# The two PSUM banks of y, split by token half instead of by channel half

## The chip, the cores and the metric

The kernel runs on one core of a Trainium2 chip. The metric is the device time of one execution in microseconds; the time given is the median of several executions. The profile beside it is that of one further execution, which has its own time.

## The reference

Two blocks follow each other. The first is a chunked state-space scan over 4 batches, 8 heads, 768 tokens, 32 channels a head and 16 states; the second mixes tokens through a low-rank product (rank 32) and then channels through two matrices with a ReLU between them. Cut to what matters here:

```python
for c in range(nc):                                  # chunks of 32 tokens
    M = einsum('bhin,bhjn->bhij', Cc, Bc) * L        # C B^T, decayed, causal
    y_intra = einsum('bhij,bhjd->bhid', M, xc)
    y_inter = einsum('bhin,bhnd->bhid', Cc, state) * decay_to_i
    y[chunk] = y_intra + y_inter
    state = decay_full * state + sum_j(Bc * xc * decay_from_j)
# mixer, on y as (batch, token, 256 channels)
u = y + (y^T U V)^T
out = u + relu(u w_ch1) w_ch2
```

## The kernel before

The kernel takes chunks of 64 tokens instead of 32. A block is 128 tokens, that is two token halves p of 64; a pair k of two blocks c is 256 tokens, and there are 12 pairs, three to a batch. All matrices are float32, and every matmul instruction leaves two records in the trace.

What is done, and in which order, is written out by hand in the string PLAN (lines 34 to 70): each word is a letter and its indices, and `follow` calls the function of that letter, so that the words give the order in which each engine gets its instructions. An engine works through its own queue in that order and waits where an operand is not there. Between the words of the scan stand those of the mixer (U, f, e, h, d, S, a, p, q) for the batch before, so that TensorE has matmuls of 128 rows and 128 columns to do meanwhile. The words B, X and w are loads issued by SyncE (SP); each is held until the last VectorE instruction that stands before it in PLAN is done, and the loads behind it in SP's queue wait with it.

The words that bear on y, for a pair k:

- `P`, `Q`: VectorE scales B and C with the decays into BC. `T`, `V`: TensorE transposes BC, ScalarE (or VectorE) copies the result into T and, masked by head, into Cm.
- `g` (`gram`, line 506): TensorE forms C B^T of the pair, 16 matmuls that use 32 rows of the array and 64 columns, into four banks (line 522). `m` and `M` (`mask`): VectorE cuts it to the causal part, M (through the helper's line, L174).
- `s` (`state`, line 546): TensorE forms B^T x per half block, 16 matmuls of 64 rows and 32 columns (line 556). `u` (`update`): VectorE carries the state S from half block to half block, GpSimd makes Sm of it, which is S masked by head.
- `n` (`intra(k, 0)`) and `j` (`crossed`, that is `intra(k, 1)`), line 680: the M x share of y, 32 matmuls of 64 rows and 32 columns, half of them in n and half in j.
- `i` (`inter`, `carried`, line 642): the states' share of y, C times Sm, 16 matmuls of 32 rows and 64 columns; 12 in the first pair of a batch, whose first half block has no state.
- `I` (`both`): i of pair k and g of pair k+1 in one word, their matmuls interleaved. PLAN has it for pairs 7, 9 and 10.
- `y` (`yout`): two ScalarE copies take y from PSUM into yT, which has channels on partitions and tokens in the free dimension. `t`, `O` (`ytokens`): TensorE transposes yT back (line 707), and the result goes into ytok.

y of a pair takes two PSUM banks. Bank n holds channel half n (heads 4n to 4n+3), and in its free dimension the two blocks, the two token halves and 64 tokens. A matmul whose operands lie on partitions 0 to 63 works in the upper rows of the array, one with operands on 64 to 127 in the lower rows. M x of token half p uses row half p. In the states' share the row half is the channel half n, since T and Sm have heads on partitions; so that share fits bank n as it is. Of M x, n does what lies straight (row half p into bank n = p), and j what lies crossed (row half p into bank n = 1 - p).

A crossed piece must not begin before the last straight matmul on these banks is done. The code keeps this order with a VectorE instruction that waits for the straight ones and that the first crossed matmul waits for: either one that does so in any case (`behind["part"]`), or a copy of one column into the tile settled that is there for nothing else (`apart`; for the last pair `settle`).

The first matmul into a bank and a group of 32 output partitions clears it (`fresh`, line 614); the later ones add.

Of the kernel before, what the change touches and what calls it, by code (L numbers as in the profile page):

```python
# [44 lines left out]
    'R4 e1.0.4 e1.0.1 f1.0.6 i6 h1.0.0 s7 R7 R6 X8 B8 j6 e1.0.5 d0.0.0.0 d0.0.0.1 d0.0.0.2 h1.0.4 '  # L45
    'u7 f1.0.7 e1.0.6 h1.0.1 h1.0.6 d0.0.0.3 T9 h1.0.5 T9 P8 d0.1.2.0 e1.0.7 h1.0.7 d0.1.2.1 f1.0.2 '
    'd0.1.1.0 e1.0.2 T8 f1.0.3 d0.1.1.1 d0.1.2.2 d0.1.2.3 e1.0.3 T8 y6 h1.0.2 h1.0.3 d0.1.1.2 '
    'd0.1.1.3 s8 u8 n7 I7 s9 j7 d1.0.0.0 d1.0.1.0 y7 m8 d1.0.0.1 d1.0.0.2 M8 d1.0.1.1 S1.1 f1.1.0 '
    'R5 d1.0.0.3 d1.0.1.2 R4 R6 X11 f1.1.7 R7 e1.1.0 h1.1.0 P11 d1.0.0.4 d1.0.1.3 d1.0.0.5 f1.1.6 '
    'e1.1.7 d1.0.1.4 u9 d1.0.2.0 d1.0.1.5 e1.1.6 h1.1.6 d1.0.2.1 f1.1.1 d1.0.2.2 d1.0.2.3 e1.1.1 '  # L50
    'h1.1.7 f1.1.4 t7 d1.0.2.4 d1.0.2.5 f1.1.3 e1.1.4 h1.1.1 f1.1.2 e1.1.3 f1.1.5 e1.1.2 h1.1.2 i8 '
    'n8 s10 j8 h1.1.3 h1.1.4 e1.1.5 d1.1.1.0 d1.1.0.0 d1.1.0.1 u10 d1.1.1.1 d1.1.1.2 d1.1.0.2 '
    'h1.1.5 d1.1.1.3 d1.1.0.3 d1.1.2.0 d1.1.2.1 d1.1.2.2 d1.1.2.3 y8 d1.1.0.4 d1.1.1.4 d1.1.1.5 '
    'd1.1.2.4 d1.1.2.5 d1.1.0.5 t8 t6 g9 T10 m9 T10 M9 p2 n9 I9 m10 q2 T11 T11 M10 j9 y9 a2.0 s11 '
    'u11 I10 m11 n10 S2.0 M11 t9 f2.0.0 f2.0.4 e2.0.0 h2.0.0 f2.0.1 f2.0.5 j10 e2.0.1 f2.0.2 y10 '
    'e2.0.5 h2.0.1 e2.0.4 h2.0.4 f2.0.3 h2.0.5 e2.0.2 i11 n11 e2.0.3 h2.0.2 h2.0.3 f2.0.6 f2.0.7 '
    'a2.1 e2.0.6 h2.0.6 j11 y11 S2.1 e2.0.7 d2.0.0.0 h2.0.7 t10 t11 d2.0.0.1 d2.0.0.2 f2.1.1 f2.1.0 '
    'd2.0.0.3 f2.1.3 e2.1.1 e2.1.0 d2.0.0.4 d2.0.0.5 p3 h2.1.0 f2.1.2 h2.1.1 d2.0.2.0 d2.0.1.0 '
    'e2.1.2 h2.1.2 d2.0.2.1 e2.1.3 h2.1.3 d2.0.1.1 d2.0.1.2 d2.0.2.2 d2.0.2.3 f2.1.5 f2.1.4 q3 '
    'e2.1.5 e2.1.4 d2.0.1.3 d2.0.2.4 h2.1.4 d2.0.2.5 d2.0.1.4 d2.0.1.5 f2.1.6 f2.1.7 h2.1.5 a3.0 '  # L60
    'e2.1.6 d2.1.0.0 e2.1.7 h2.1.6 a3.1 d2.1.2.0 d2.1.2.1 d2.1.0.1 d2.1.0.2 S3.0 f3.0.3 f3.0.2 '
    'h2.1.7 f3.0.0 d2.1.0.3 e3.0.3 f3.0.1 d2.1.0.4 d2.1.0.5 e3.0.2 h3.0.2 h3.0.3 e3.0.0 d2.1.1.0 '
    'd2.1.2.2 d2.1.2.3 d2.1.1.1 d2.1.1.2 f3.0.5 f3.0.4 d2.1.1.3 e3.0.1 h3.0.0 h3.0.1 d2.1.2.4 '
    'e3.0.5 f3.0.6 e3.0.4 d2.1.1.4 f3.0.7 d2.1.2.5 h3.0.4 e3.0.6 e3.0.7 h3.0.6 d2.1.1.5 d3.0.2.0 '
    'S3.1 d3.0.2.1 d3.0.0.0 d3.0.0.1 d3.0.0.2 f3.1.4 h3.0.5 f3.1.0 h3.0.7 d3.0.2.2 f3.1.5 e3.1.4 '
    'd3.0.2.3 e3.1.0 h3.1.0 f3.1.1 d3.0.2.4 d3.0.0.3 f3.1.2 d3.0.0.4 d3.0.0.5 d3.0.2.5 d3.0.1.0 '
    'h3.1.4 e3.1.5 h3.1.5 e3.1.1 h3.1.1 f3.1.6 d3.0.1.1 f3.1.3 e3.1.2 e3.1.6 d3.0.1.2 e3.1.3 h3.1.2 '
    'h3.1.3 d3.0.1.3 f3.1.7 d3.0.1.4 d3.0.1.5 h3.1.6 e3.1.7 d3.1.2.0 d3.1.2.1 d3.1.2.2 h3.1.7 '
    'd3.1.2.3 d3.1.1.0 d3.1.1.1 d3.1.2.4 d3.1.2.5 d3.1.1.2 d3.1.1.3 d3.1.0.0 d3.1.0.1 d3.1.0.2 '
    'd3.1.0.3 d3.1.1.4 d3.1.1.5 d3.1.0.4 d3.1.0.5 ')  # L70


@with_exitstack
def kernel(
# [27 lines left out]
    nc = tc.nc  # L102
    P = 128
# [13 lines left out]
    Q = 32  # L117
    H = 64
# [44 lines left out]
    class Kept:  # L163
# [6 lines left out]
        def __getattr__(self, name):  # L170
# [8 lines left out]
    vector = Kept(nc.vector)  # L179
# [7 lines left out]
        out=a_sb,  # L187
        in_=a.rearrange("(g b) h (c s) -> g (b h c) s", g=2, s=P).rearrange(
            "g r s -> r g s"))
# [322 lines left out]
    def opened(k, tags="xxzz"):  # L512

        st[k].setdefault("of", {})["g"] = behind["turn"]
        st[k]["g"] = four(tags, 2, 2, H)

    def crossing(k, c, p, of):

        s = st[k]
        for r in of:  # L520
            rows, cols = ts(r, Q), ts(p, H)
            nc.tensor.matmul(  # L522
                out=s["g"][r][cols, c], lhsT=s["T"][rows, 0, c, cols],
                rhs=s["Cm"][rows, :, :, ts(2 * c + p, Q)].rearrange("r v t i -> r v i t"),
                start=(c == 0), stop=True, skip_group_check=True)
# [67 lines left out]
    def apart(copy):  # L593

        behind["part"] = op = copy(out=settled, in_=slot[:, :1])
        for product in behind["first"]:
            tc.add_manual_dep(op.ins, product.ins.name, mybir.DependencyInfo(
                mybir.DependencyClass.Sync, mybir.DependencyReason.DATA))

    def settle():  # L600

        t = bank("x", P)
        nc.tensor.matmul(out=t, lhsT=ident, rhs=ident, start=True, stop=True)
        behind["part"] = vector.tensor_copy(out=settled, in_=t[:, :1])

    def channels(k):

        s = st[k]
        if "y" not in s:
            s["y"] = [bank("y", 2, 2, H) for n in range(2)]  # L610
            s["seen"] = set()
        return s["y"]

    def fresh(k, n, quadrants):

        new = {(n, i) for i in quadrants}
        seen = st[k]["seen"]
        assert new <= seen or not new & seen
        first = not new <= seen
        seen |= new  # L620
        return first

    def straight():

        behind.pop("part", None)
        behind["turn"] += 1

    def inter(k):

        channels(k)  # L630
        straight()
        for c in range(2):
            for p in range(2):
                carried(k, c, p, range(4))

    def carried(k, c, p, of):

        b, q = pairs[k]
        own = st.get(("Sm", b, 4 * q + 2 * c + p))
        assert own is not None or 4 * q + 2 * c + p == 0  # L640
        for r in of if own is not None else ():
            behind["first"].append(nc.tensor.matmul(  # L642
                out=channels(k)[r // 2][ts(r % 2, H), c, p], lhsT=own[ts(r, Q)],
                rhs=st[k]["T"][ts(r, Q), 1, :, ts(2 * c + p, Q)].rearrange("r t i -> r i t"),
                start=fresh(k, r // 2, range(2 * (r % 2), 2 * (r % 2) + 2)),
                stop=True, skip_group_check=True))

    def both(k):

        channels(k)  # L650
        straight()
        opened(k + 1)
        for c in range(2):
            for v in range(2):
                carried(k, c, 0, (v, v + 2))
                crossing(k + 1, 0, c, (1 - v, 3 - v))
                carried(k, c, 1, (v, v + 2))
        for p in range(2):
            crossing(k + 1, 1, p, range(4))

    def intra(k, part):

        s = st[k]
        y = channels(k)
        after = None
        if part == 0:
            straight()
        else:  # L670
            if "part" not in behind:
                apart(vector.tensor_copy)
            after = behind.pop("part")
            behind["first"] = []
        for c in range(2):
            for p in range(2):
                n = (p + part) % 2
                for i in range(4):
                    h, half = 4 * n + i, ts(p, H)
                    product = nc.tensor.matmul(  # L680
                        out=y[n][ts(i, Q), c, p], lhsT=x_sb[k][half, c, h],
                        rhs=s["M"][half, h // 2, c, h % 2], start=fresh(k, n, [i]),
                        stop=True, skip_group_check=True)
                    if part == 0:
                        behind["first"].append(product)
                    if after is not None:
                        tc.add_manual_dep(
                            product.ins, after.ins.name, mybir.DependencyInfo(
                                mybir.DependencyClass.Sync, mybir.DependencyReason.DATA))
                        after = None  # L690

    def yout(k):
        b, q = pairs[k]
        if q == 0 and b:
            yT[b] = mix.tile([P, NCB, S], FP32, tag="yT", name="yT")
            ytok[b] = mix.tile([P, NC, DM], FP32, tag="ytok", name="ytok")
        for n in range(2):
            nc.scalar.copy(out=yT[b][:, n, ts(q, 2 * P)],
                           in_=st[k]["y"][n].rearrange("p c v i -> p (c v i)"))

    def ytokening(k, tag="w", copies=None):

# [204 lines left out]
        for _ in range(2):  # L907
            next(t)

    def crossed(k):  # L910

        if k + 1 == len(pairs) and "part" not in behind:
            settle()
        intra(k, 1)

    def ytokens_of(k, v):
        ytokens(k, *(("x",), ("z", (vector.tensor_copy,) * 2), ("w",))[v])

    scans = dict(P=prep, T=turned, g=gram, s=state, m=lambda k: mask(k, (0, 1)),
                 M=lambda k: mask(k, (2, 3)), u=update, i=inter, I=both, n=lambda k: intra(k, 0),  # L920
                 j=crossed, y=yout, t=ytokens, Q=lambda k, c: prep(k, c, 1),
                 O=ytokens_of,
                 V=lambda k, c, v: turn(k, c, 1, "wx"[v // 2], vector if v % 2 else None))
    whole = dict(c=convert, C=lambda n: convert(-1), R=refined, A=lambda i: decays(every_batch, "w", [i]),
# [58 lines left out]
```

## Time and profile before

| | |
|---|---|
| median of 3 runs | 224.13 us (224.01 to 224.38) |
| the profiled execution, its own time | 224.41 us |
| its span, first to last instruction | 222.6 us |
| granted TensorE clock, mean | 0.999 |
| L680, M x: matmul records, mean | 768, 223 ns |
| L642, states' share: matmul records, mean | 352, 235 ns |
| L522, C B^T: matmul records into the x and z banks | 192 and 192, 305 and 306 ns |
| L698, copies of y | 24, 382 ns |
| copies into settled | 9, median 154 ns |

The durations of matmul records overlap, since several small ones work in different parts of the array at once; what a group costs is read from the start of its first record to the start of the next group. PE in the profile is TensorE's matmuls, PEld its weight loads, DVE is VectorE, ACT ScalarE, POOL GpSimd, SP SyncE. Times in the timelines are microseconds from the start of the span.

### The profile page before, as it was taken

The numbers are of one execution on the slowest core, as the hardware profiler recorded it, in microseconds if no ns is written. First come the engines' busy times: TensorE is split into PE (matmuls) and PEld (weight loads), VectorE is DVE, ScalarE is ACT, GpSimd is POOL, SyncE is SP. The second block draws the span as 40 slices with busy tenths as digits, with TensorE's granted clock in tenths as the row PEclk, the third lists the DMA queues.
The fourth block names the chain that finished last, engine by engine and source line by source line (L and its number), as shares of the span: only waits on it lengthen the run. The fifth ranks groups of instructions, "written<-read, shape, count | busy, mean of one in ns | idle before, by whom it ended". The sixth has DMA issues, their size and how long they took to land.

```text
span 222.6 us, 7025 instructions
## 1 busy us (share of the span) xinstructions
PE 215.5 (97%) x3022; PEld 182.2 (82%) x3022; DVE 146.4 (66%) x314; ACT 108.7 (49%) x251; POOL 32.7 (15%) x44
## 2 busy tenths in 40 slices
PE   7999999999999999999999999999999999999994
PEld 4666566665668888889999996788999999999993
DVE  4688498568657755737955736959863955674921
ACT  3334745675668075543444214476535455553510
POOL 3012223405577053000010100000000000000000
PEclk9999999999999999999999999999999999999999
DMA  6968888898633446100120010000000100101011
GB/s 102 129 98 144 138 158 189 187 281 113 134 47 71 84 57 91 37 24 28 27 71 27 3 49 27 3 3 3 0 27 1 47 0 27 47 0 50 6 43 50
DMA packets 69520, 14.59 MB, mean 66 GB/s; under 512 B 63792, under 2 KB 67696, under 8 KB 69488
## 3 DMA queue, kind: packets, MB, share of 16 engines
q1 hardware_dynamic: 69488, 14.13, 32.3%
q8 instruction: 24, 0.39, 0.8%
q14 instruction: 8, 0.07, 0.1%
HBM read 10.98 MB, written 3.15 MB: 63 GB/s over the span
## 4 chain that ended last, share of the span: by engine, by line
PE 89%; DVE 5%; DMA 2%; SPq 2%; ACT 1%; issue 1%; POOL 0%; POOLq 0%
PE x L790 31%; PE z L790 24%; PE y L790 12%; PE y L680 3%; PE x L522 2%; PE y L642 2%; PE w L482 2%; DMA bc<-in_B_dram 2%; DVE M L174 2%; PE w L707 2%; SPq L202 2%; PE w L556 1%; PE x L136 1%; PE z L522 1%; PE w L734 1%; PE w L136 1%
## 5 line engine op out<-in xcount | busy, mean ns | idle before, releaser
L790 PE MATMUL z<-u,w 128*128 128x384 f32 x144 | 33.6, 347 | 0.0
L790 PE MATMUL x<-u,w 128*128 128x384 f32 x144 | 32.7, 344 | 0.5 <-DVE u L174 0.3
L174 DVE SCALAR_TENSOR_TENSOR words<-words 128x768 fp32r<-128x768 f32 (+3 forms) x35 | 29.5, 846 | 1.4
L790 PEld LDWEIGHTS x<-u,w 128*128 128x128 f32 x144 | 24.8, 188 | 1.8 <-DVE u L174 0.7
L795 ACT ACTIVATE x<-x 128x384 f32<-128x384 f32 (+1 forms) x30 | 13.6, 454 | 25.1 <-PE x L790 18.2
L790 PEld LDWEIGHTS z<-u,w 128*128 128x128 f32 x144 | 24.1, 189 | 0.9
L790 PE MATMUL x<-w2c,words 128*128 128x256 f32 x112 | 22.3, 339 | 0.0
L795 ACT ACTIVATE z<-z 128x384 f32<-128x384 f32 (+1 forms) x27 | 12.6, 466 | 18.6 <-PE z L790 18.6
L790 PE MATMUL y<-w,words 128*128 128x256 f32 x144 | 19.8, 283 | 0.0
L790 PEld LDWEIGHTS x<-w2c,words 128*128 128x128 f32 x112 | 18.3, 189 | 1.5
L174 DVE SCALAR_TENSOR_TENSOR words<-x,words 128x384 fp32r<-128x384 f32 x24 | 13.3, 554 | 9.3 <-ACT words L825 9.2
L790 PEld LDWEIGHTS y<-w,words 128*128 128x128 f32 x144 | 18.8, 190 | 0.3
L583 POOL TENSOR_TENSOR Sm<-S,own 128x256 f32<-128x256 f32 (+1 forms) x12 | 7.6, 634 | 76.4 <-DVE S L174 48.0
L174 DVE SCALAR_TENSOR_TENSOR words<-z,words 128x384 fp32r<-128x384 f32 x24 | 13.2, 552 | 5.2 <-ACT words L825 5.1
L825 ACT ACTIVATE words<-z 128x384 fp32r<-128x384 f32 x24 | 11.7, 491 | 10.1 <-PE z L790 10.0
L825 ACT ACTIVATE words<-x 128x384 fp32r<-128x384 f32 x24 | 11.8, 493 | 5.3 <-PE x L790 5.0
L790 PE MATMUL x<-w,words 128*128 128x256 f32 x96 | 14.2, 285 | 0.0
L790 PEld LDWEIGHTS x<-w,words 128*128 128x128 f32 x96 | 12.9, 190 | 0.2
L680 PEld LDWEIGHTS y<-M,x 64*32 64x32 f32 x768 | 8.1, 105 | 5.7 <-issue 3.0
L174 DVE TENSOR_TENSOR BC<-bc,F 128x512 f32<-128x512 f32 (+2 forms) x18 | 9.4, 535 | 4.7 <-DMA bc<-in_B_dram 3.2
L680 PE MATMUL y<-M,x 64*32 64x64 f32 x768 | 12.0, 223 | 0.4 <-DVE settled L174 0.3
L174 DVE SCALAR_TENSOR_TENSOR S<-S,kept,w 128x64 f32<-128x64 f32 x40 | 11.2, 279 | 1.6
(149 smaller groups left out, 411.9 us busy)
## 6 DMA issues: line engine op xcount, KB each, us to landing
words<-in_moe_w_ch_dram SPq DMA_DIRECT2D x7, 512.0 KB, 5.0
x<-in_x_dram SPq DMA_DIRECT2D x24, 128.0 KB, 3.7
out_dram<-ytok SPq DMA_DIRECT2D x24, 128.0 KB, 1.7
bc<-in_B_dram SPq DMA_DIRECT2D x24, 64.0 KB, 3.3
bc<-in_C_dram SPq DMA_DIRECT2D x12, 128.0 KB, 3.4
words<-in_moe_w_ch_dram SPq DMA_DIRECT2D x2, 256.0 KB, 3.8
words<-in_moe_U_dram SPq DMA_DIRECT2D x1, 192.0 KB, 2.9
words<-in_moe_V_dram SPq DMA_DIRECT2D x4, 48.0 KB, 2.8
```

The source lines that it names most:

```text
L136: nc.tensor.matmul(out=t[:, :m * P].rearrange("p (m i) -> p m i", i=P), lhsT=ident, rhs=ident[:, None, :].to_broadcast([P, m, P]), start=T ...
L174: self.last = call(*args, **kwargs)
L202: op = issuer[0].dma_start(**kwargs)
L482: nc.tensor.transpose(out=tp[:, i, v], in_=s["BC"][:, i, c + v].rearrange("p h n -> p (h n)"), identity=ident)
L522: nc.tensor.matmul(out=s["g"][r][cols, c], lhsT=s["T"][rows, 0, c, cols], rhs=s["Cm"][rows, :, :, ts(2 * c + p, Q)].rearrange("r v t i -> ...
L583: nc.gpsimd.tensor_tensor(out=s["Sm"][:, sl], in0=s["S"][:, sl].rearrange("p i (s d) -> p i s d", s=2), in1=own2[:, b, 4 * q + sl.start:4 ...
L642: behind["first"].append(nc.tensor.matmul(out=channels(k)[r // 2][ts(r % 2, H), c, p], lhsT=own[ts(r, Q)], rhs=st[k]["T"][ts(r, Q), 1, :, ...
L680: product = nc.tensor.matmul(out=y[n][ts(i, Q), c, p], lhsT=x_sb[k][half, c, h], rhs=s["M"][half, h // 2, c, h % 2], start=fresh(k, n, [i] ...
L707: nc.tensor.transpose(out=t[:, c, g], in_=yT[b][:, g, ts(2 * q + c, P)], identity=ident)
L790: nc.tensor.matmul(out=t, lhsT=lhsT, rhs=rhs, start=start, stop=True, skip_group_check=True)
L795: nc.scalar.activation(t, t, AF.Copy, scale=1.0 + EPS)
L825: nc.scalar.activation(gs[j, m // 2][0][:, m % 2], t, AF.Relu, scale=NEAR)
```

## The change

The banks of y are now split by token half: bank p holds token half p, and in its free dimension the two blocks, the two channel halves and 64 tokens.

- M x of token half p uses row half p, so all 32 matmuls lie straight. `n` is now all of M x in one piece; its `part` is gone.
- The states' share, whose row half is the channel half n, now has a straight half (n = p) in `i` and a crossed half (n = 1 - p) in `j` (the new function `across`), 8 matmuls each, 6 each in the first pair of a batch. The crossed half waits as the crossed half of M x did.
- `both`, the interleaved word I, is gone. In PLAN `I7` becomes `i7 g8`, `I9` becomes `i9 g10`, `I10` becomes `i10 g11`, and `j` is moved to stand behind that g in two of these: `n7 I7 s9 j7` becomes `n7 i7 g8 j7 s9`, and `j9`, which stood behind `m10 q2 T11 T11 M10`, now stands ahead of them. VectorE gets one more copy into settled, ahead of the mask of pair 10.
- The two copies of `yout` take one token half each, of both channel halves, and write it into yT in four runs of 64 tokens.

Nothing else is moved in PLAN; the rest of its lines differ in where they break.

```diff
-... d0.1.1.3 s8 u8 n7 I7 s9 j7 d1.0.0.0 ...
+... d0.1.1.3 s8 u8 n7 i7 g8 j7 s9 d1.0.0.0 ...
...
-... p2 n9 I9 m10 q2 T11 T11 M10 j9 y9 a2.0 s11 u11 I10 m11 n10 S2.0 M11 ...
+... p2 n9 i9 g10 j9 m10 q2 T11 T11 M10 y9 a2.0 s11 u11 i10 g11 m11 n10 S2.0 M11 ...
...
     def inter(k):
         channels(k)
         straight()
-        for c in range(2):
-            for p in range(2):
-                carried(k, c, p, range(4))
+        carried(k, 0)
...
+    def carried(k, part, after=None):
+        b, q = pairs[k]
         for c in range(2):
             for v in range(2):
+                for p in range(2):
+                    own = st.get(("Sm", b, 4 * q + 2 * c + p))
...
+                    n = (p + part) % 2
+                    r = 2 * n + v
                     product = nc.tensor.matmul(
+                        out=channels(k)[p][ts(v, H), c, n], lhsT=own[ts(r, Q)],
+                        rhs=st[k]["T"][ts(r, Q), 1, :, ts(2 * c + p, Q)].rearrange(
+                            "r t i -> r i t"),
+                        start=fresh(k, p, range(2 * v, 2 * v + 2)),
                         stop=True, skip_group_check=True)
...
+    def across(k):
+        if "part" not in behind:
+            if k + 1 == len(pairs):
+                settle()
+            else:
+                apart(vector.tensor_copy)
+        after = behind.pop("part")
+        behind["first"] = []
+        carried(k, 1, after)
+
+    def intra(k):
+        s = st[k]
+        y = channels(k)
+        straight()
+        for c in range(2):
+            for n in range(2):
+                for p in range(2):
+                    for i in range(4):
+                        h, half = 4 * n + i, ts(p, H)
+                        behind["first"].append(nc.tensor.matmul(
+                            out=y[p][ts(i, Q), c, n], lhsT=x_sb[k][half, c, h],
+                            rhs=s["M"][half, h // 2, c, h % 2], start=fresh(k, p, [i]),
+                            stop=True, skip_group_check=True))
...
-        for n in range(2):
-            nc.scalar.copy(out=yT[b][:, n, ts(q, 2 * P)],
-                           in_=st[k]["y"][n].rearrange("p c v i -> p (c v i)"))
+        out = yT[b][:, :, ts(q, 2 * P)].rearrange("r n (c p i) -> r p c n i", c=2, p=2)
+        for p in range(2):
+            nc.scalar.copy(out=out[:, p], in_=st[k]["y"][p])
...
-                 M=lambda k: mask(k, (2, 3)), u=update, i=inter, I=both, n=lambda k: intra(k, 0),
-                 j=crossed, y=yout, t=ytokens, Q=lambda k, c: prep(k, c, 1),
+                 M=lambda k: mask(k, (2, 3)), u=update, i=inter, n=intra, j=across, y=yout, t=ytokens, Q=lambda k, c: prep(k, c, 1),
```

## The prediction

> **What bounds the kernel now.** I read the profile's page first, then the chain of waits, then the timelines of TensorE and VectorE around every place where y is built.
>
> ```profile
> span 222.6 us, 7025 instructions
> ...
> PE 215.5 (97%) x3022; PEld 182.2 (82%) x3022; DVE 146.4 (66%) x314; ACT 108.7 (49%) x251; POOL 32.7 (15%) x44
> ...
> PEclk9999999999999999999999999999999999999999
> ...
> PE 89%; DVE 5%; DMA 2%; SPq 2%; ACT 1%; issue 1%; POOL 0%; POOLq 0%
> ```
>
> TensorE is busy 97% of the span at full granted clock and is 89% of the chain that ended last. Going through its timeline, I find after 32.2 us only four pauses above 0.04 us: 0.17 at 78.3, 0.05 at 135.9, 0.10 at 138.8 and 0.34 at 143.4. So behind 32 us a change is worth what it does to TensorE's own time, unless it meets one of these pauses. Before that another chain rules:
>
> ```profile
> 14.29 0.74 DVE M L174 x2
> 15.03 0.54 DVE BC L174 x2
> ...
> 15.99 1.39 SPq L202
> ...
> 19.61 4.09 DMA bc<-in_B_dram
> 23.72 0.69 DVE BC L174
> 24.55 0.46 PE y L680 x32
> ```
>
> A load of B for pair 3 lands at 23.7 us, VectorE scales it, and only then, in the same queue, comes the small copy into settled that frees the crossed piece of pair 2. TensorE time saved before 24.55 us is lost there.
>
> **Prices.** Every matmul here leaves two records (L680: 384 instructions, 768 records). From TensorE's timeline at pair 11 and at pair 8 (start, length of the group, records):
>
> ```profile
> 149.99 0.78 PE L642 MATMUL y<-T,Sm 32*64 32x64 f32 x32
> 150.70 0.45 PE L680 MATMUL y<-M,x 64*32 64x64 f32 x32
> 151.09 0.44 PE L790 MATMUL z<-u,w 128*128 128x384 f32 x1
> ```
> ```profile
> 121.59 0.45 PE L680 MATMUL y<-M,x 64*32 64x64 f32 x32
> 121.85 0.59 PE L556 MATMUL w<-x,BC 64*32 64x64 f32 x32
> 122.38 0.46 PE L680 MATMUL y<-M,x 64*32 64x64 f32 x32
> 122.77 0.44 PE L790 MATMUL z<-u,w 128*128 128x384 f32 x1
> ```
>
> Start to start, a whole states' share costs 0.71 us (149.99 to 150.70); the 24 records of pair 6 cost 0.57 (83.10 to 83.67), so eight records are 0.14, and half a share of 16 records is 0.43, of 12 records 0.36. Half of M x (32 records) costs 0.39 (150.70 to 151.09). Of each about 0.15 is the emptying of the array before another shape; M x into a neighbour of the same shape takes 0.26 (121.59 to 121.85). The doubtful price is a piece of 64 records, which before never has running undisturbed: the second 32 small matmuls of one shape take 0.53 at pair 8 (121.85 to 122.38) though they are the same size, 0.38 without the emptying; at pair 3 it is 0.52 (38.40 to 38.91), at pair 7 0.55 (102.69 to 103.24). So 64 records cost 0.39 + 0.38 = 0.77, as much as the two halves apart. At the pace of the first 32 it would be 0.63. I take 0.77, since three places show the slow second half and none a fast one; 0.63 stays as the lower end.
>
> [...]
>
> **The change, part by part** (pair k; n is M x, i the states' share, g the next C B^T, j the crossed piece, s the state's products).
>
> Start, pairs 0 and 1: n0 grows by 0.38, g1 and its masks come that much later, and so does the scaling of B and C that w0's load is held for. That ends at 15.22 and the load is issued at 15.56 because the queue is busy with V until 15.45; 15.22 + 0.38 + 0.04 is 15.64, so SP's chain, and with it 24.55, moves +0.08 (bounds 0 and +0.38, if nothing of it is covered). What pairs 0 and 1 change otherwise ends in the wait at 24.55.
>
> Pair 2: the crossed piece is 16 records of the share instead of 32 of M x: +0.04. The transposes for t2 now need both copies of y, since each copy fills a token half of both channel banks: they run at 25.56, 25.84, 26.00 and 26.11, the first between the copies' ends at 25.51 and 25.79; now all four follow the second: +0.10. Sum +0.14 (0.05 to 0.20). The copies themselves keep their 256 columns; ScalarE's T copy of the same size into two runs takes the same 0.37 us as L698.
>
> Pair 3: n3 is fed by masks until 30.1, then has some 44 records left, which end about 0.1 after the wait for ps at 30.57 that hides it now: +0.10 (0 to +0.38). i3's saving goes into g4's wait for ScalarE. j3 with s4 costs 0.79 now (38.13 to 38.91); then j3 adds 0.21 behind g4 and s4 alone 0.39: -0.19. Sum -0.1 (-0.3 to +0.2).
>
> Pair 4: i4 -0.28, n4 +0.38, j4 +0.05 (0.43 for 0.38): +0.15. Pair 8, the same: +0.15. Pair 11: 0.43 + 0.77 + 0.43 against 0.71 + 0.39 + 0.39: +0.14. With fast second halves each would be 0.
>
> Pair 5: 57.16 to 59.23, 2.07 now. n5 0.77, and i5, g6, j5 in one run of one shape, priced as i5 with g6 now (1.26), with 0.07 less emptying: 1.19. -0.11 (-0.25 to 0).
>
> Pair 6: n6 +0.10, as 0.77 from 77.60 ends at 78.37 and VectorE frees the next matmul at 78.27 (0 at the fast pace); i6 -0.21; s7 and j6 0.81 now, then 0.39 + 0.36: -0.06. Sum -0.17.
>
> Pair 7, the interleaved I gone: n7 +0.38 behind s8; I7 1.37 (101.06 to 102.42) becomes 1.19; s9 and j7 0.81 become s9 alone, 0.39. Sum -0.22 (-0.4 to 0).
>
> Pairs 9 and 10:
>
> ```profile
> 140.07 0.53 PE L642 MATMUL y<-T,Sm 32*64 32x64 f32 x3
> ...
> 141.68 0.46 PE L680 MATMUL y<-M,x 64*32 64x64 f32 x32
> ...
> 143.41 1.82 PE L790 MATMUL x<-u,w 128*128 128x384 f32 x8 [0.34 <-DVE u L174]
> ```
> ```profile
> 141.73 0.76 DVE L174 TENSOR_TENSOR M<-x,causal 128x256 int32<-128x256 int32 x2 [0.44 <-PE z L522]
> ```
>
> n9 waits for its mask (135.42) and g10 for Cm (135.90), so its growth is largely hidden and q2 stays near 137.18; j9 is moved past q2, T11 and both masks of 10, and leaves idle time before L762, which waits for ps either way: 0. The added settled copy (0.15) falls into VectorE's 1.81 us idle before 137.23. In pair 10 the interleaved I10 lasts 1.61 us, its mask waits until 141.73 and L790 for u until 143.41. Apart, i10 waits for y9's second copy (140.28) and starts its last matmul near 140.56; g11 takes 0.52 more and ends its last near 141.43: mask and u 0.29 earlier. n10, 0.77, then ends where it does now, so most of the 0.34 us pause is gained: -0.29 (-0.34 to 0). j10: +0.05.
>
> Sum: +0.08 +0.14 -0.10 +0.15 -0.11 -0.17 -0.22 +0.15 +0 -0.29 +0.05 +0.14 = -0.18 us. The profiled execution took 224.41 us, of it 222.6 span and 1.8 around it; so 222.4 and 224.2. The median run is 0.28 below the profiled one: 223.95, say 223.9. 0.2% of the time is 0.45 us, about what a measurement can tell from no change; this lies inside.
>
> **Rivals.** First, **one straight piece at its opening pace**: 64 records in 0.63. That takes 0.14 off in each of pairs 4, 5, 7, 8 and 11, 0.1 in 3 and 6 and the 0.08 at the start: -0.98, 222.9 us. For it: the first 32 records run 6 to 7 ns apart, and n has the same shape throughout. Against: the second halves named above. [...]
>
> Second, the other side: **the crossed piece waits where g no longer covers settled**.
>
> ```profile
> L174 DVE COPY settled<-slot x9: 144/154/154, 16.1 to 122.2; 128x1 f32<-128x1 f32 x9
> ```
>
> Between the straight and the crossed half lie the end of i (0.23 behind its last start), the copy (0.15) and about 0.11 of semaphores: 0.49. g offers 0.66. In pairs 3, 5 and 7, j now stands right behind g. It decides when VectorE's queue is held by another instruction for more than 0.17 us as i ends; its mean one is 146.4/314 = 0.47 us, so up to 0.30 each, 0.9 in all; with every straight second half at pair 7's slower 0.43 it is 0.9 + 8 x 0.05 = +1.3, less 0.2: 225.2; half of it 224.6. Against: at 37.47, 58.39 and 102.25 VectorE was idle before settled now, 0.31, 1.75 and 0.48 us.
>
> Third, **the interleaving was worth more than it looks**, or pair 10's pause stays because u waits for something else: without pair 7's 0.18 and pair 10's 0.29 it is 224.4, no change.
>
> **Chances.** Forecast, gains and losses cancel (223.5 to 224.4): 0.38, its own range. Third rival, 0.14, mostly within 0.2%. First rival, 0.26, faster. Second, 0.22, slower. Faster by over 0.2% (below 223.7) gets the first rival and a quarter of the forecast's lower side, 0.36; slower (above 224.6) the second and part of the third, 0.26; same 0.38. The range 222.9 to 225.0 leaves about 2 in 10 out.
>
> **What would show it.** Right: L680's successor in groups of 64 records, at pair 11 about 0.77 us to the next L790; halves of 16 records at 0.43; the pause before L790 near 143 below 0.1; 78.3's pause gone; j2 still bound by settled near 24.6. Wrong: 64 records in 0.63 (first rival), or waits for settled on TensorE or its weight loads in pairs 3, 5, 7 (second). A pause that is new in the gapless part, or a start moved by more than 0.1 at 24.55, would show a cost I have not seen.

## The result, and the profile after

The changed kernel took 225.49 us (median of 14 runs, 224.83 to 226.44), the kernel before on the same chip 224.33 us (14 runs, 223.67 to 224.43): ratio 1.0059, 95% interval 1.0045 to 1.0074. (The ratio is not exactly the quotient of the two medians: by the medians the loss is 1.2 us, by the ratio 1.3.) The forecast was 223.9, no change; the kernel became slower, and its times scatter more. The profiled execution is the slowest of the 14: 226.44 us with a span of 224.7.

From the page of the changed kernel:

```profile
span 224.7 us, 7028 instructions
...
PE 216.1 (96%) x3022; PEld 183.8 (82%) x3022; DVE 147.2 (65%) x315; ACT 108.5 (48%) x251; POOL 32.2 (14%) x44
...
q8 instruction: 24, 0.39, 0.7%
...
PE 94%; DVE 3%; issue 1%; ACT 1%; POOL 0%; POOLq 0%
```

TensorE has the same 3022 matmuls and is busy 0.6 us more; the span is 2.1 us longer, so most of it is time in which TensorE does nothing. TensorE's groups of the changed kernel name the places (busy time, mean ns | idle time ahead of the group and what ended it):

```profile
L784 PE MATMUL x<-u,w 128*128 128x384 f32 x144 | 33.0, 345 | 0.4 <-issue 0.4
...
L646 PE MATMUL y<-T,Sm 32*64 32x64 f32 x352 | 12.6, 238 | 0.4 <-DVE settled L174 0.4
...
L556 PE MATMUL w<-x,BC 64*32 64x64 f32 x352 | 6.0, 224 | 0.9 <-issue 0.9
...
L756 PE MATMUL x<-Vs,ps 128*128 128x384 f32 x8 | 3.1, 387 | 0.5 <-DVE ps L174 0.5
```

Two pauses end by "issue": TensorE waited for nothing that the profile shows. TensorE's timeline of the changed kernel at both:

```profile
49.22 0.86 PE L681 MATMUL y<-M,x 64*32 64x64 f32 x64
49.88 0.48 PE L556 MATMUL w<-x,BC 64*32 64x64 f32 x22
51.22 0.30 PE L556 MATMUL w<-x,BC 64*32 64x64 f32 x2 [0.86 <-issue]
51.44 2.85 PE L784 MATMUL z<-yT,w1f 128*128 128x384 f32 x8
```
```profile
143.02 0.86 PE L681 MATMUL y<-M,x 64*32 64x64 f32 x64
143.81 0.65 PE L701 MATMUL w<-ident,yT 128*128 128x128 f32 x4
144.22 1.02 PE L784 MATMUL x<-u,w 128*128 128x384 f32 x3
145.68 1.64 PE L784 MATMUL x<-u,w 128*128 128x384 f32 x7 [0.44 <-issue]
```

The first stops within s5, all of whose matmuls have the same operands: 22 records go through, then 0.86 us nothing, then the last two. A wait for data would have stopped the first. In the kernel before s5 runs through:

```profile
48.98 0.51 PE L680 MATMUL y<-M,x 64*32 64x64 f32 x32
49.29 0.49 PE L556 MATMUL w<-x,BC 64*32 64x64 f32 x24
49.72 3.06 PE L790 MATMUL z<-yT,w1f 128*128 128x384 f32 x8
```

The second takes the place of the 0.34 us wait for u.

The prices at pairs 11 and 8, to be held against the two stretches shown of before:

```profile
152.12 0.50 PE L646 MATMUL y<-T,Sm 32*64 32x64 f32 x16
152.55 0.86 PE L681 MATMUL y<-M,x 64*32 64x64 f32 x64
153.34 0.62 PE L784 MATMUL z<-u,w 128*128 128x384 f32 x2
```
```profile
122.32 0.50 PE L646 MATMUL y<-T,Sm 32*64 32x64 f32 x16
122.75 0.86 PE L681 MATMUL y<-M,x 64*32 64x64 f32 x64
123.41 0.51 PE L556 MATMUL w<-x,BC 64*32 64x64 f32 x32
123.86 0.50 PE L646 MATMUL y<-T,Sm 32*64 32x64 f32 x16
124.29 0.62 PE L784 MATMUL z<-u,w 128*128 128x384 f32 x2
```

Start to start, 64 records of M x cost 0.79 us ahead of another shape and 0.66 ahead of the same one, half a share 0.43; the prices were 0.77, 0.64 (0.26 and 0.38) and 0.43. And the chain of waits at the start:

```profile
14.68 0.74 DVE M L174 x2
15.41 0.53 DVE BC L174 x2
...
23.85 0.80 PE y L681 x53
24.65 0.02 issue
24.68 0.17 DVE settled L174
24.84 0.04 issue
24.89 0.57 PE y L646 x16
```

The crossed piece of pair 2 begins at 24.89 instead of 24.55, and the chain no longer comes there over the load of B and its scaling: ahead of it stands mostly TensorE's own work up to n2, and settled behind that.

### The profile page after: what moved, and what is told of

The parts are those of the page before. It is cut to its first block, busy times and chain, and to the rows that moved or that the text cites. A ratio compares the mean times of both kernels' runs of the same rounds, so it can differ in the third digit from the quotient of the medians.

```text
span 224.7 us, 7028 instructions
## 1 busy us (share of the span) xinstructions
PE 216.1 (96%) x3022; PEld 183.8 (82%) x3022; DVE 147.2 (65%) x315; ACT 108.5 (48%) x251; POOL 32.2 (14%) x44
## 4 chain that ended last, share of the span: by engine, by line
PE 94%; DVE 3%; issue 1%; ACT 1%; POOL 0%; POOLq 0%
PE x L784 31%; PE z L784 24%; PE y L784 12%; PE y L681 4%; PE y L646 4%; PE x L522 2%; PE w L701 2%; PE w L482 2%; PE x L136 1%; PE w L556 1%; PE z L522 1%; PE w L728 1%; PE w L136 1%; PE w L746 1%; DVE M L174 1%
## 5 line engine op out<-in xcount | busy, mean ns | idle before, releaser
L784 PE MATMUL x<-w2c,words 128*128 128x256 f32 x112 | 22.3, 339 | 0.0
L646 PE MATMUL y<-T,Sm 32*64 32x64 f32 x352 | 12.6, 238 | 0.4 <-DVE settled L174 0.4
L646 PEld LDWEIGHTS y<-T,Sm 32*64 32x64 f32 x352 | 8.9, 131 | 4.5 <-issue 2.0
L174 DVE TENSOR_TENSOR ytok<-y,ytok 128x256 f32<-128x256 f32 x9 | 3.8, 424 | 12.5 <-PE y L784 12.4
```

Of the source, the lines that this page charges most:

```text
L174: self.last = call(*args, **kwargs)
L646: product = nc.tensor.matmul(out=channels(k)[p][ts(v, H), c, n], lhsT=own[ts(r, Q)], rhs=st[k]["T"][ts(r, Q), 1, :, ts(2 * c + p, Q)].rear ...
L784: nc.tensor.matmul(out=t, lhsT=lhsT, rhs=rhs, start=start, stop=True, skip_group_check=True)
```

## What the pauses have in common

I matched the 920 matmuls of the mixer (U, f, e, h, d and so on) one by one in both traces and took the differences of their starts. The shift is +0.59 at 30.6 us of before, +0.45 at 38.9, +1.72 at 49.7, +1.51 at 51.7, +1.45 at 103.9, +1.53 at 122.8, +2.09 at 143.9, +2.12 at 153.4, and stays there. The two jumps are the two pauses. This is the trace of the slowest of 14 runs, so the 2.1 us, and the size of its pauses, are more than the 1.2 us that the medians differ by.

Then I counted TensorE's records (weight loads, matmuls and its few semaphore instructions) in the order of their starts, from 0. The first record behind the one pause is number 1985 = 7 x 256 + 193, behind the other 4801 = 18 x 256 + 193. (Where the 193 comes from no run shows.) The page's line q8, an instruction queue, has 24 packets, 0.39 MB or 16,384 bytes each, which is 64 bytes for each of 256 records. I number the packets as they come on this queue; "the end of packet 7" is, in the expectations too, the place 7 x 256 + 193 in TensorE's records, where it needs the seventh of them. Packet 7 began its transfer at 48.85 us, 2.36 us before TensorE went on, packet 18 at 143.13, 2.55 us before. The DMA view of the changed kernel for 48.7 to 49.9 us shows packet 7 in its surroundings (packets, MB, share of the 16 engines):

```profile
q1 hardware_dynamic: 519, 0.40, 102.3%
q8 instruction: 1, 0.02, 4.8%
```

In the kernel before, record 1985 falls into j4, 7.2 us after packet 7 began its transfer, and record 4801 comes 5.3 us after packet 18.

Theory A: TensorE's instructions come in packets of 256; a packet is asked for only about when TensorE enters the one ahead of it, and is usable some 2.4 us after its transfer begins. Where some 250 records pass in less than 3 to 4 us, as in a burst of small matmuls, and the end of a packet falls there, TensorE stands still. The change moved the ends of packets 7 and 18 into bursts. Theory B: the loss is the longer start and the new order's own terms. Theory C: the pauses are waits that belong to s5 and to pair 10's new order.

## The experiments

Each is given with its median, and its ratio to the kernel before on the same chip with the 95% interval.

**Moving the ends of the packets, at the start of the kernel.** Small matmuls that nobody reads are added to the fillers, the matmuls with the identity that the function `idle` issues at the start:

```diff
+    tiny = iter([(0, 0), (0, 5)])            # pad20; (wide units less, small ones more) per filler
+                # pad128: [(0, 0), (0, 0), (1, 8), (1, 8), (0, 0), (1, 8), (1, 8)]
     def idle(t, n):
+        wide, count = next(tiny, (0, 0))
+        n -= wide
+        for i in range(count):
+            nc.tensor.matmul(out=t[ts(i % 4, Q), :H], lhsT=ident[:H, ts(i % 4, Q)],
+                             rhs=ident[:H, :H], start=True, stop=True)
```

after_pad20: 

> The changed kernel with 5 extra small matmul instructions (20 TensorE records) near 3.5 us, where TensorE waits for VectorE anyway. Theory A: TensorE's instructions arrive in packets of 16 KB (24 packets on the instruction queue, 256 records each), and the two pauses that the profile puts down to issue (1.07 us in s5 at 51 us, 0.45 us at 145 us) lie where the record count reaches 7 x 256 + 193 and 18 x 256 + 193, because a burst of small matmuls reached the end of a packet before the next was there. Shifting the records by 20 moves both ends of packets out of the bursts: the issue pauses go, and the time falls by 0.5 to 1.2 us against the changed kernel, to 224.3 to 225.0 us (ratio to before 1.000 to 1.003). Theory B, that the whole loss is the longer start and the new order: nothing changes, 225.3 to 225.6 us. Theory C, that the pauses are waits of the new order (settled, u): they stay at s5 and at pair 10, 225.3 to 225.6 us.

after_pad128: 

> The changed kernel with 32 extra small matmul instructions (128 records) in place of 4 of the wide filler matmuls in the first 13 us, which take about the same time. Theory A: the ends of packets now fall into the bursts of pair 7 (near 103 us, where 288 records pass in 2.3 us) and of pair 9 (near 137 us, 3.6 us): issue pauses there, at record counts of 193 more than a multiple of 256, and none in s5 and at pair 10; 225 to 227.5 us, not below 225. Theories B and C: no change in the places of the pauses, 225.3 to 225.6 us, or up to 0.3 us more if the filling is not free.

before_pad128: 

> The kernel before with the same 32 small matmul instructions (128 records) in place of 4 wide fillers. Nothing of the change is in it. Theory A: an end of a packet falls near 102.7 us, into n7 and I7 where 288 records pass in 2.4 us; an issue pause of 0.5 to 1.5 us is new there, at 193 more than a multiple of 256, and the time is 224.7 to 226 us (ratio 1.002 to 1.007). Theories B and C: 224.0 to 224.4 us, no new pause.

before_pad20: 

> The kernel before with 5 extra small matmul instructions (20 records) near 3.5 us: the control for the price of the padding. Theory A: no packet ends in a burst, so no issue pause, and 224.1 to 224.5 us. Theories B and C: the same. If it is slower by 0.3 us or more, the padding itself costs time and the other runs have to be read against this one.

Measured: after_pad20 226.51 us (1.0095, 1.0079 to 1.0111), after_pad128 229.81 (1.0243, 1.0219 to 1.0267), before_pad128 227.81 (1.0182, 1.0152 to 1.0212), before_pad20 225.06 (1.0039, 1.0022 to 1.0056).

All four times lie above what was expected, and the control shows one reason: before_pad20 has no such pause and lies 0.6 to 0.7 us behind from 30.6 us on, so the padding delays the start. In after_pad20, 20 records were too few: both pauses are there, 0.84 and 0.75 us from record to record, s5 now stopping 20 records earlier. But the places are as theory A says. before_pad128, which has nothing of the change, stops at pair 7:

```profile
106.04 0.45 PE L563 MATMUL w<-x,BC 64*32 64x64 f32 x32
106.31 0.21 PE L687 MATMUL y<-M,x 64*32 64x64 f32 x1
107.43 0.46 PE L687 MATMUL y<-M,x 64*32 64x64 f32 x31 [0.91 <-issue]
107.82 0.74 PE L797 MATMUL x<-w,words 128*128 128x256 f32 x4
```

The record at 107.43 is number 3521 = 13 x 256 + 193; one matmul of j7 is through, the next 31 have the same operands. The pauses of this kind over 0.3 us in the four traces and in that of the changed kernel, each at 193 more than a multiple of 256:

| kernel | record | packet's transfer begins | TensorE goes on | between |
|---|---|---|---|---|
| changed | 1985, 4801 | 48.85, 143.13 | 51.21, 145.68 | 2.36, 2.55 |
| after_pad20 | 1985, 4801 | 49.55, 142.62 | 51.77, 144.97 | 2.22, 2.35 |
| before_pad128 | 961, 1217, 3521 | 21.69, 26.08, 105.08 | 23.94, 28.36, 107.43 | 2.25, 2.29, 2.36 |
| after_pad128 | 961, 1217, 3521, 4545 | 22.12, 25.90, 105.32, 138.98 | 24.46, 28.33, 107.81, 141.99 | 2.34, 2.44, 2.49, 3.01 |

So theory C falls: padding takes the pauses away from s5 and pair 10 (after_pad128 has neither) and makes them in the kernel before. By the matched matmuls of before_pad128 the stop at pair 7 costs 0.95 us, and this is not made up: the shift is +3.63 us from 30.6 us to pair 7 and +4.58 from there to the end. What the two pauses of the change are worth these four don't tell, since the padding costs time itself.

**The same where it costs nothing, and two parts of the change undone.** The small matmuls now stand in front of v (line 880), in the bank that v writes next; v9 has 9 of them, 36 records. `g1` puts g1 and m1 ahead of n0, `j9` puts j9 back to where it stood:

```diff
         v = [bank(tag, NC * RK) for tag in "yyxz"]
+        for i in range(9):
+            nc.tensor.matmul(out=v[0][ts(i % 4, Q), :H], lhsT=ident[:H, ts(i % 4, Q)],
+                             rhs=ident[:H, :H], start=True, stop=True)
...
-... X1 F5 F3 n0 YB2 g1 m1 YV0 ...
+... X1 F5 F3 g1 m1 n0 YB2 YV0 ...              (after_v9_g1)
...
-... g10 j9 m10 q2 T11 T11 M10 y9 ...
+... g10 m10 q2 T11 T11 M10 j9 y9 ...           (after_v9_j9)
```

before_v9: 

> The kernel before with 9 extra small matmul instructions (36 TensorE records) in front of v (21 us), where TensorE waits for a ScalarE copy anyway. Control for the next three. Counting 256 records back from each end of a packet in the trace of before, no end of a packet then comes sooner than 3.8 us after the last one (4.2 us before 32 us): theory A, no issue pause. The place is free if 24.55 us stays within 0.1 us. All theories: 224.1 to 224.6 us. Dearer: the padding costs time here too.

after_v9: 

> The changed kernel with the same 36 records in front of v, where TensorE waits 0.65 us. Theory A: the ends of packets 7 and 18 move 36 records earlier, out of the bursts at 51 and 145 us, to where 256 records take 3.8 us and more; no issue pause over 0.2 us. What is left is the change without them, the start (+0.35) and the pairs' own terms: +0.3 to +0.7 us against before_v9, 224.5 to 225.1 us (225.5 for the changed kernel alone). Theories B and C: as the changed kernel, 225.3 to 225.7 us, with pauses at s5 and pair 10.

after_v9_g1: 

> As after_v9, with g1 and m1 ahead of n0 in the plan, so that the longer n0 delays neither the masks of pair 1 nor the scaling of B and C that holds w0's load. Theory B, that the start is worth 0.35 us: 24.9 us goes back to 24.55 and the time falls by 0.3 us against after_v9, to 224.2 to 224.8. Rival: the start is bound by something else that n0 delays too (j0, y0, the banks), and nothing is gained or up to 0.2 us lost.

after_v9_j9: 

> As after_v9, with j9 back at its place in the plan before the change, behind both masks of pair 10. My working put the move of j9 at 0; the traces show +0.10 us at pair 9 and +0.40 at n10. If the move is what costs there, 0.1 to 0.3 us is gained against after_v9; if not, within 0.1 us of it.

Measured: before_v9 224.40 us (1.0002, 0.9993 to 1.0011): the padding is free. after_v9 224.89 (1.0034, 1.0017 to 1.0051), 0.6 below the changed kernel; the pause behind pair 10 is gone, that in s5 is smaller (0.59 from record to record, again number 1985). after_v9_g1 225.78 (1.0076, 1.0043 to 1.0108): worse, with new stops at records 449 and 705 (0.58 and 0.31 from record to record) and a wait of 0.60 us for x at 22.3 us. So it gains nothing, but with these stops in it it doesn't tell what the longer start is worth; the sharper form of theory B follows below. after_v9_j9 224.79 (1.0007, 0.9979 to 1.0034): by the time unclear; its trace has a smaller stop in s5 (0.29); by the matched matmuls the shift changes at pair 10 by -0.35 us where after_v9 has -0.14, so j9's old place is worth 0.21.

**More padding, j9, and M x of pair 0 in two pieces.** v10 is 10 small matmuls. `n0` gives `intra` an optional block, and PLAN one piece on either side of g1, as before the change:

```diff
-    def intra(k):
+    def intra(k, *only):
...
-        for c in range(2):
+        for c in only or range(2):
...
-... F3 n0 YB2 g1 m1 YV0 ...
+... F3 n0.0 YB2 g1 m1 n0.1 YV0 ...
```

after_v10: 

> The changed kernel with 40 extra records in front of v (after_v9 had 36, and still a pause of 0.59 us at record 7 x 256 + 193, where the packet's transfer began late). With 40 the end of packet 7 comes 4.8 us after that of packet 6, and the shortest distance elsewhere is 3.4 us. Theory A: no issue pause at all; what is left is the new order itself, +0.2 to +0.3 us against before_v9 (the +0.66 of after_v9's trace less the 0.44 that its pause cost): 224.4 to 224.9 us. Theory C, that the pause in s5 belongs to s5: it is there again, 224.8 to 225.2.

after_v10_j9: 

> As after_v10 with j9 back at its place before the change, which also takes the added settled copy out of VectorE's queue ahead of the mask of pair 10. after_v9's trace gave -0.14 us at the matmuls behind pair 10 against the kernel before, after_v9_j9's -0.35. So 0.2 us less than after_v10: 224.2 to 224.6. Rival: the 0.2 us is used up by a later wait, same as after_v10.

after_v10_j9_n0: 

> As after_v10_j9 with M x of pair 0 in two pieces of 32 records, one ahead of g1 as before the change and one behind m1. Theory B in its sharper form: the 32 records more ahead of g1 delay the masks, the scaling and w0's load by 0.3 us; then 24.9 us comes back to 24.5 and 0.2 to 0.35 us is gained, 223.9 to 224.3 us, at or below the kernel before. Rival: the start differs by 0.3 us from one execution to the next in any case (24.38 to 25.0 us in the traces of after so far) and n0 has little part in it: within 0.1 us of after_v10_j9.

after_j9: 

> The changed kernel with j9 back and no extra records: the packets end where they do in the changed kernel. Theory A: both issue pauses stay (record 7 x 256 + 193 in s5 and 18 x 256 + 193 behind pair 10), and at most the 0.2 us of j9 is gained: 225.1 to 225.6 us, 0.6 us or more above after_v10_j9. Theory C, that the pause behind pair 10 came from the order around j9: it goes, 224.8 to 225.1.

Measured: after_v10 224.85 us (1.0025, 1.0009 to 1.0042), after_v10_j9 224.54 (1.0017, 1.0003 to 1.0030), after_v10_j9_n0 224.35 (1.0015, 0.9997 to 1.0032), after_j9 225.27 (1.0055, 1.0030 to 1.0080). after_j9 has both pauses (0.89 and 0.79 from record to record), as A says, and gains only 0.2. (Its trace, of its slowest run, has besides a wait of 0.91 us for a mask near 40 us, which is not of this kind.) In the traces of after_v10_j9 and after_v10_j9_n0 the pause in s5 is still there (0.60 and 1.17), against my expectation: the end of packet 6 was passed at 44.96, but packet 7 began its transfer only at 47.97 and 48.60. My count took the request to lead to a transfer within about a us; in this stretch up to 3.6 lie between the end of one packet and the transfer of the next.

**s5 taken off the end of the packet.**

```diff
-... R1 s5 U0.1.3 B10 M5 U0.1.5 X9 ...
+... R1 U0.1.3 B10 M5 U0.1.5 s5 X9 ...
```

after_U: 

> The changed kernel with s5 put behind the four matmuls U0.1.3 and U0.1.5 instead of ahead of them (PLAN only; nothing added or taken away). The end of packet 7 stays at record 7 x 256 + 193, but is now reached about 2.8 us later, near 53 us, when packet 7 is there (its transfer starts at 48.9 in the trace of the changed kernel, 49.8 at the latest in all the traces so far). Theory A: the 1.07 us pause near 51 us goes, the one behind pair 10 stays: 0.6 to 1.0 us less than the changed kernel, 224.5 to 224.9 us. Rival C, that s5 waits for something of its own: the pause moves along with s5, 225.3 to 225.6.

before_U: 

> The kernel before with the same move of s5. No end of a packet falls there, so theory A: no gain, 224.1 to 224.5 us. If the order is better by itself, it is faster here too, and the gain of after_U counts for nothing.

after_v10_U (with v10): 

> The changed kernel with the 40 records in front of v (no pause behind pair 10) and s5 behind U (no pause near 51 us): the change without the two pauses. By the traces +0.66 us at the end in after_v9 less 0.44 of its pause near 51: +0.2 to +0.4 against before_v9, 224.4 to 224.8 us. If it is still 0.8 us above the kernel before, the pauses explain only their own part and the rest of my terms is off by as much.

after_all (with v10, j9 and n0): 

> after_v10_j9_n0 (40 records in front of v, j9 back, M x of pair 0 in two pieces) with s5 behind U: every cost found so far taken out. after_v10_j9_n0 took 224.35 us and its trace had a pause of 1.17 us near 51 us, 0.6 to 1.0 of which should go: 223.5 to 223.9 us, 0.2 to 0.3% below the kernel before. Rival: pauses are made up by a later wait, 224.2 or more.

Measured: after_U 225.14 us (1.0041, 1.0026 to 1.0056), before_U 224.82 (1.0032, 1.0015 to 1.0048), after_v10_U 225.14 (1.0041, 1.0028 to 1.0055), after_all 224.60 (1.0023, 1.0011 to 1.0035). In after_U the pause near 51 us is gone, though s5 is the same (the other one is there, 0.34 from record to record, and costs 0.14 by the matched matmuls), but the control says that the move itself costs 0.53 us: by the matched matmuls of before_U s5 takes 0.45 us in its new place, while U0.1.3, now first in line, comes only 0.06 sooner, since it has to wait for a mask, its bank being one that g5 wrote (0.16 us; s5 hid that). So the times of after_U, after_v10_U and after_all, expected at 224.5 to 224.9, 224.4 to 224.8 and 223.5 to 223.9, all lie higher. Against before_U, after_U and after_v10_U are 0.32 us slower, after_all is 0.22 us faster.

**Fewer records instead of more.** v's 16 matmuls become 8:

```diff
+    pick = const.tile([P, 2, 4, Q], FP32)     # pick[:, v] is the identity in the quarters q = v, v + 2
...
-        for q in range(4):
+        for q in range(2):
             for i in range(4):
                 rows = ts(i, Q)
-                nc.tensor.matmul(out=v[i][ts(q, Q)], lhsT=ident[rows, rows],
+                nc.tensor.matmul(out=v[i], lhsT=pick[rows, q].rearrange("p q r -> p (q r)"),
                                  rhs=Vq[rows] if q % 2 else Vn[rows].bitcast(FP32),
-                                 start=True, stop=True, skip_group_check=True)
+                                 start=q == 0, stop=True, skip_group_check=True)
```

after_s8: 

> The changed kernel with the 16 small matmuls of v (32 rows, 32 output partitions) made into 8 (32 rows, 128 output partitions, even and odd quarters picked by a constant, added up in PSUM; the same result): 32 records fewer, so that every later end of a packet lies 32 records later in the work. For packet 7 that is near 53 us, among matmuls of 384 columns, and for packet 18 near 146 us; counted back in the traces, no end then comes sooner than 3.9 us after the last. Nothing is put into TensorE's way and s5 stays where it is. Theory A: neither pause; what is left is the change itself, +0.2 to +0.4 us by the traces: 224.4 to 224.7 us. If it stays at 225.2 or more, the two pauses are not what the change lost.

after_j9_n0_s8: 

> The same with j9 back and M x of pair 0 in two pieces: every cost found taken out, without the 0.5 us that moving s5 cost (before_U). after_all stood 0.2 us below before_U: 223.9 to 224.2 us, about 0.1% below the kernel before. Rival: what is gained at pair 10 is lost at the start, 224.3 to 224.6.

Measured: after_s8 224.56 us (1.0009, 0.9996 to 1.0023), after_j9_n0_s8 224.19 (0.9993, 0.9981 to 1.0006). TensorE's timeline of after_s8 at the two places of the pauses:

```profile
49.38 0.86 PE L686 MATMUL y<-M,x 64*32 64x64 f32 x64
50.04 0.49 PE L561 MATMUL w<-x,BC 64*32 64x64 f32 x24
50.46 2.99 PE L789 MATMUL z<-yT,w1f 128*128 128x384 f32 x8
```
```profile
142.96 0.66 PE L706 MATMUL w<-ident,yT 128*128 128x128 f32 x4
143.37 2.38 PE L789 MATMUL x<-u,w 128*128 128x384 f32 x10
```

s5's 24 records run through, and so do the ten behind pair 10, with no wait for u either. Against the changed kernel the matched matmuls gain 1.15 us at the first place and 0.72 at the second. By the ratios, 0.50% of the time, 1.1 us, of the 0.59% that the change lost is gone, with 32 records less ahead of these places. The kernel before with this form of v was not run; but in the trace of after_s8 the matched matmul at 30.6 us of before, behind v, lies at +0.76, later than the +0.59 of the changed kernel, so the gain isn't made at v.

With j9 and n0 undone too, the kernel comes out level with the one before; the interval holds 1, so it isn't shown to beat it.

## Why the prediction was wrong, step by step

**The step that failed** is the first one: "So behind 32 us a change is worth what it does to TensorE's own time, unless it meets one of these pauses." It took TensorE's instructions to be there whenever its operands are. The two pauses that came of that, in pairs 4 and 10, make up 0.9 of the 1.2 us by the medians, 1.1 of the 1.3 by the ratios (the changed kernel against after_s8). None of my rivals held this mechanism; what I had named as the sign of a cost not seen, a pause that is new in the gapless part, is what came. I had passed it over though the page of before has the queue's line with its 24 packets. In the burst of small matmuls the next packet came too late: ahead of the first pause the 256 records of a packet passed in 1.8 us (48.35 to 50.14), and TensorE went on 2.36 us after the next packet's transfer had begun. In the kernel before, where 7.2 us lie between that transfer's start and the same record, there is no stop.

**The terms**, read in after_s8, which has no pauses, by the steps of the shift against the kernel before:

| | predicted | after_s8 |
|---|---|---|
| pair 3, j3 and s4 | -0.19 | -0.14 |
| pair 4 | +0.15 | +0.10 |
| pair 5 | -0.11 | -0.03 |
| pair 6 | -0.17 | 0.00 |
| pair 7 | -0.22 | -0.09 |
| pair 8 | +0.15 | +0.09 |
| pairs 9 and 10 | -0.29 | -0.15 |
| j10 and pair 11 | +0.19 | +0.06 |
| sum behind 32 us | -0.49 | -0.16 |

The signs are right but for pair 6, where nothing is gained: a half share of 12 records costs 0.42 us, as much as one of 16, where I had 0.36. At pair 7 the shift falls by 0.19, nearly as predicted, but 0.12 is given back behind s9.

**j9, put at 0, costs 0.21.** I wrote that moving it "leaves idle time before L762, which waits for ps either way". The idle time is there, but q2 (L746, in these two L751), with which the chain to ps begins, was pushed back by j9. TensorE's timeline of after_s8, where j9 (the first line) stands ahead of q2:

```profile
137.54 0.49 PE L651 MATMUL y<-T,Sm 32*64 32x64 f32 x12
137.96 0.70 PE L751 MATMUL w<-pT,spot 128*128 128x256 f32 x2
138.50 0.60 PE L487 MATMUL w<-ident,BC 128*128 128x128 f32 x4
139.59 0.44 PE L761 MATMUL x<-Vs,ps 128*128 128x384 f32 x1 [0.49 <-DVE ps L174]
```

and of after_j9_n0_s8, where it is back:

```profile
136.73 0.70 PE L751 MATMUL w<-pT,spot 128*128 128x256 f32 x2
137.26 0.60 PE L487 MATMUL w<-ident,BC 128*128 128x128 f32 x4
137.79 0.49 PE L651 MATMUL y<-T,Sm 32*64 32x64 f32 x12
138.35 0.44 PE L761 MATMUL x<-Vs,ps 128*128 128x384 f32 x1
```

From q2 to the matmul that needs ps it is 1.63 and 1.62 us; j9 fits into that time for nothing, and costs when it stands ahead of it.

**The start** was put at +0.08 for pairs 0 and 1, with bounds 0 and 0.38. M x of pair 0 in two pieces gained 0.19 us (after_v10_j9 to after_v10_j9_n0) and, with j9's 0.21 taken off, 0.16 (after_s8 to after_j9_n0_s8); both differences lie within the intervals. The start also differs from one execution to the next: the crossed piece of pair 2 begins at 23.83 to 24.55 us in three traces of the kernel before (as it is, with v9, with U), at 24.28 to 24.96 in eight of the changed one with n0 whole, and at 24.03 to 24.72 in three with n0 in two pieces. The means, 24.24, 24.69 and 24.38, put the start up to this place at about +0.45, where my sum had +0.08 (pair 2's own +0.14 comes behind it), and n0's part of it at 0.3. Without before_U, whose trace is of its fastest run, the mean of before is 24.45 and the start +0.25. So the term was too small by 0.2 to 0.4, and that is as exactly as these runs tell it.

**The rivals.** The first fell with the price: 0.79 us, not 0.63. The second, waits for settled in pairs 3, 5 and 7, didn't show: the 0.4 us in the profile after are two waits of the start, 0.19 at 16.73 us and 0.25 at pair 2. That its 225.2 us lies near the result is luck. The third was in part right: pair 7 gave 0.09 where I had 0.22. At pair 10 the wait for u did go, and the shift of the changed kernel falls by 0.25 between the matmuls at 138.8 and 143.4 us of before; then the second pause takes 0.71. With the pauses out, the change comes to +0.2 us (interval -0.1 to +0.5) where I had -0.18.

## What to carry to other kernels

Where TensorE works through hundreds of short matmuls, count its records: find the ends of the instruction packets in the trace (here 256 records apart), and see which burst they fall into before and after a change. A stop in the middle of like instructions, put down to nothing, is the sign (0.86 us within s5). Here 128 small records in place of four wide fillers made such a stop in the kernel before (0.91 us at pair 7), and 32 records less took two away from the changed one, with 0.50% of the time; so a loss or gain of 0.5% is the change's own only if it stays when the instructions are shifted. For a piece moved into idle time, see where the awaited chain begins: behind q2, with which it begins here, j9 was free, and ahead of it it cost 0.21 us.

## What the runs showed of the hardware that was not expected

- The stops of TensorE that end by "issue" in the middle of like instructions lie at 193 more than a multiple of 256 records, and the 24 packets of the instruction queue have 16,384 bytes each, 64 bytes for each of 256 records; that TensorE's instructions come in packets of 256 is read from these two. The stops at the packets' ends lasted until 2.2 to 2.6 us after the next packet's transfer began, with three exceptions: 3.0 us in after_pad128, 3.4 in after_v9_j9 and 3.7 in after_v9_g1 at record 705, whose packets were 1.6, 2.0 and 2.2 us on their way instead of about one, as in the other stops. Counted from the end of the transfer there is no exception: in the 20 stops of 0.29 us and more in all the traces TensorE went on 1.26 to 1.56 us after the packet's transfer had ended, and in no trace did a packet's first record start sooner than 1.26 us after it. In all the traces a transfer began at the earliest 297 records ahead of the place where the packet was needed.
- The transfer of packet 7 began 0.5 us after the end of packet 6 in the changed kernel, with loads on all DMA engines (the 102.3% shown), and 3.6 us after it in after_v10_j9_n0, where loads took 77% of the engines' time meanwhile. Why it began so late stays open. That the loads hold it up is not shown: in after_v10_j9_n0 nothing at all was transferred from 46.11 to 46.55 us, within those 3.6 us, and still packet 7 began only at 48.60. When TensorE asks for a packet the traces don't tell.
- Ahead of another shape, 64 small matmul records of M x take 0.79 us where 32 take 0.39, and a share of 12 records takes as long as one of 16 (0.42 and 0.43). What fills the time ahead of another shape, which the prediction calls the emptying of the array, no trace shows; the difference is what was measured (in the kernel before 0.39 us for 32 records at pair 11, against 0.26 ahead of the same shape at pair 8).
- That a crossed piece must wait for the straight ones is the order that both kernels keep (at pair 2 it begins behind settled, at 24.55 and 24.89 us). No run leaves this order out, so what would come without it is not shown.
